# Shifting every right-hand tile of a fused retention and mixture-of-experts kernel by 32 bytes

## The chip, the cores and the metric

One core of one Trainium2 chip runs the whole program. The metric is the device time of one execution in microseconds (us). Engines are named as in the profile: PE is TensorE's matmul, PEld its weight load, DVE is VectorE, ACT is ScalarE, POOL is GpSimd and SP is SyncE, which issues the DMAs. On-chip memory (SBUF) has 128 partitions; a tile occupies the same byte range in each of them, and "address" below means the place in that range.

## The reference

Three stages follow each other on 1536 tokens (2 batches of 768) of width 512. Inputs and outputs are float32.

```python
# retention, 8 heads of width 64
state = gamma * state + outer(k[t], v[t])
y[t] = scale * q[t] @ state
# first layer, 512 -> 2048 -> 512
h = x @ w_in
x = (h * np.clip(h + 3.0, 0.0, 6.0) / 6.0) @ w_out
# second layer, 8 experts of 512 -> 1024 -> 512, all of them for each token
P = np.exp(x @ w_gate - max)
for _ in range(8):
    P /= P.sum(1, keepdims=True) + 1e-09
    P /= P.sum(0, keepdims=True) + 1e-09
    P *= N / E
for e in range(E):
    out += P[:, e:e + 1] * (np.maximum(x @ w1[e], 0.0) @ w2[e])
```

## The kernel before

A float32 product is made of three fp32r matmuls: each operand is split into a part `hi` and a rest `lo`, and hi·hi, hi·lo and lo·hi are added up in PSUM. A matmul takes its stationary operand (the weights, 128 x 128) by a weight load and then streams the moving operand, 512 or 384 columns wide. The order of all work is written by hand (`tc.manual_schedule`); each engine runs its instructions in that order.

The retention runs over 12 chunks of 128 tokens (`scores`, `attend`, `state`), and its output goes into `xhi`/`xlo`, one pair of tiles for each of three blocks of 512 tokens. The first layer has 48 steps: three groups of 4, 6 and 6 weight slices, and in each group blocks 0, 1 and 2 after one another. A step has 12 matmuls at L357 (`stage_a`: moving `xhi`/`xlo`, weights `whi`/`wlo`) and 12 at L387 (`stage_b`: moving `ghi`/`glo`, weights `whi`/`wlo`), all of them 512 columns wide; L357 runs two steps ahead. Its weights arrive as float64 and are split by DVE and ACT (`splitting`, L157 to L174) between the steps.

The second layer has two halves of 768 tokens, and for each 32 pairs of intermediate slices (64 in all). A pair makes 7 products of a Strassen-like scheme at L597 (`product`: 6 matmuls each, 384 columns, moving `xh`/`xl`, weights `w1hi`/`w1lo`), and between them come the matmuls at L672 (`outputs`: 512 columns, moving `w2hi`/`w2lo`, weights `gh`/`gl`) of the pairs before, 36 to a pair; the first two pairs have none beside them. DVE adds each finished L672 result into `o` (L685).

Tiles come from pools that take their bytes from the left or from the right end of the partition, in the order in which they are opened. The places in the built program of the kernel before are:

| side | pools and tiles | first byte of a tile, modulo 64 |
|---|---|---|
| left | `xo` (`x2`, `o`), `xa` (`xhi`, `xlo` of blocks 0 and 1: 43968, 52160, ...), `xf` (`xh`, `xl`), `m` (`raw0`, `s`, `w1hi`, `w1lo`) | 0 |
| left | the retention's `rs`, `qk`, `kv`, `a`, `ks`, `qs`, behind two tiles whose sizes are no multiples of 64 | 32 |
| right, from byte 229344 downwards | `sp` (`raw`, `w`, `t`), `xb` (`xhi`, `xlo` of block 2: 194528, 202720), `wp` and `wx` (`whi`, `wlo`), `gp` (`ghi`, `glo`), `m2` (`raw1`, `p`, `u`, `gh`, `gl`, `w2hi`, `w2lo`) | 32 |

`wx` is closed and `xf` and `m` are opened in the last block of the first layer; `m2` takes the place of `gp`, `wp`, `xb` and `sp` after the first layer. A tile that lies on bytes of an earlier one waits for that one's last reader.

Of the kernel before, what the change touches and what calls it, by code (L numbers as in the profile page):

```python
# [9 lines left out]
F32 = mybir.dt.float32  # L10
# [10 lines left out]
P = 128  # L21
# [34 lines left out]
def kernel(  # L56
# [20 lines left out]
    def pool(name, side, **kw):  # L77
        open_[name] = c = ExitStack()
        ctx.callback(c.close)
        return c.enter_context(tc.tile_pool(name=name, side=side, **kw))  # L80
# [2 lines left out]
    sk = pool("sk", "left", bufs=2)  # L83
    xo = pool("xo", "left", bufs=NU)
    xa = pool("xa", "left", bufs=NBLK - 1)
    sp = pool("sp", "right", bufs=3)
    xb = pool("xb", "right", bufs=1)
    wp = pool("wp", "right", bufs=NW)
# [826 lines left out]
```

## Time and profile before

| | before |
|---|---|
| median of 3 runs | 1346.34 us (1342.72 to 1346.85) |
| the profiled execution | 1346.3 us, span of its instructions 1344.5 us |
| PE busy | 98% of the span, 6766 matmuls |
| DVE busy | 68% |
| ACT busy | 42% |
| DMA | 99.69 MB on the hardware queue, 21.8% of 16 engines |
| granted TensorE clock | 0.999 |

Times in the views are microseconds from the first instruction of the span. A busy time of PE is modelled from pipelined matmuls, so that two neighbours overlap in it; how long a matmul holds the stream is the distance from its start to the next one's. The chain of waits is followed back from the last instruction, at each step to what released it; a piece "PE h L357 x12" is twelve matmuls at line 357 in a row, with the time from the first one's start to the start of the next piece.

### The profile page before, as it was taken

The page shows a single profiled execution, that of the slowest core. Times are in us where ns is not written, and L with a number is a line of the kernel's source. Part 1 is how long each engine was busy: PE and PEld are TensorE (multiplying, and loading weights), DVE is VectorE, ACT ScalarE, POOL GpSimd, SP SyncE. Part 2 cuts the span into 40 slices and gives each one's busy share as a digit, 9 for nine tenths or more (in the row PEclk, how much of TensorE's full clock was granted, in tenths as well). Part 3 has the DMA queues.
Part 4 walks back from the last instruction along what each step waited for, and adds up shares of the span by engine and source line. Part 5 has one row for each costly group of instructions (what it writes and reads, how often), then busy time and mean ns, then how long its engine had stood idle before and what let it go on. Part 6 is the DMA issues. An engine that isn't in the chain of part 4 may idle for free.

```text
span 1344.5 us, 17308 instructions
## 1 busy us (share of the span) xinstructions
PE 1323.4 (98%) x6766; PEld 1163.8 (87%) x6766; DVE 909.3 (68%) x1704; ACT 564.5 (42%) x1068; POOL 32.7 (2%) x34
## 2 busy tenths in 40 slices
PE   7899999999999999999999999999999999999998
PEld 6788788887888999999999998899999999999997
DVE  6866667438778666666666667766666666666663
ACT  3555545324543434433434434443443443443440
POOL 5300000000000000000000000000000000000000
PEclk9999999999999999999999999999999999999999
DMA  8622213000311111212111211311121211121201
GB/s 299 220 67 90 79 59 98 0 0 19 124 63 64 63 63 67 75 66 77 63 63 66 77 64 62 126 63 63 64 78 63 79 63 63 63 79 63 79 16 47
DMA packets 45533, 100.79 MB, mean 75 GB/s; under 512 B 3590, under 2 KB 4102, under 8 KB 45452
## 3 DMA queue, kind: packets, MB, share of 16 engines
q1 hardware_dynamic: 45452, 99.69, 21.8%
q8 instruction: 53, 0.87, 0.3%
q14 instruction: 28, 0.23, 0.1%
HBM read 96.53 MB, written 3.15 MB: 74 GB/s over the span
## 4 chain that ended last, share of the span: by engine, by line
PE 87%; DVE 7%; ACT 3%; issue 1%; DMA 1%; SPq 0%; ACTq 0%
PE acc L672 37%; PE h L597 33%; PE acc L387 8%; PE h L357 8%; ACT raw L164 1%; DVE raw L163 1%; DVE w L169 1%; DMA raw<-in_wf 1%; DVE w L159 1%; DVE a L297 0%; ACT t L365 0%; DMA raw<-in_we 0%; DVE xl L513 0%; DVE w1lo L513 0%; DVE w L157 0%
## 5 line engine op out<-in xcount | busy, mean ns | idle before, releaser
L597 PE MATMUL h<-xh,w1hi 128*128 128x384 f32 x896 | 302.0, 337 | 2.2 <-ACT p L616 1.5
L672 PE MATMUL acc<-w2hi,gl 128*128 128x512 f32 x768 | 301.7, 393 | 0.0
L597 PE MATMUL h<-xh,w1lo 128*128 128x384 f32 x896 | 301.1, 336 | 0.0
L597 PE MATMUL h<-xl,w1hi 128*128 128x384 f32 x896 | 300.6, 336 | 0.0
L672 PE MATMUL acc<-w2hi,gh 128*128 128x512 f32 x768 | 299.6, 390 | 0.0
L672 PE MATMUL acc<-w2lo,gh 128*128 128x512 f32 x768 | 298.8, 389 | 0.0
L685 DVE SCALAR_TENSOR_TENSOR o<-acc,pm,o 128x512 f32<-128x512 f32 x174 | 130.6, 750 | 143.8 <-PE acc L672 143.8
L597 PEld LDWEIGHTS h<-xh,w1hi 128*128 128x128 f32 x896 | 168.3, 188 | 21.7 <-ACT p L616 2.7
L597 PEld LDWEIGHTS h<-xl,w1hi 128*128 128x128 f32 x896 | 168.2, 188 | 19.4
L672 PEld LDWEIGHTS acc<-w2hi,gl 128*128 128x128 f32 x768 | 144.2, 188 | 30.9
L597 PEld LDWEIGHTS h<-xh,w1lo 128*128 128x128 f32 x896 | 168.2, 188 | 0.0
L672 PEld LDWEIGHTS acc<-w2lo,gh 128*128 128x128 f32 x768 | 144.3, 188 | 13.0
L672 PEld LDWEIGHTS acc<-w2hi,gh 128*128 128x128 f32 x768 | 143.9, 187 | 13.0
L616 ACT ACTIVATE p<-h 128x384 f32<-128x384 f32 x128 | 63.0, 492 | 202.9 <-PE h L597 202.8
L513 DVE TENSOR_TENSOR w1lo<-raw,w1hi 128x512 fp32r<-128x512 f32 (+1 forms) x128 | 71.1, 555 | 77.7 <-ACT w1hi L512 77.6
L513 DVE TENSOR_TENSOR w1lo<-s,w1hi 128x512 fp32r<-128x512 f32 x128 | 88.0, 688 | 38.5 <-ACT w1hi L512 38.3
L616 ACT ACTIVATE u<-h 128x384 f32<-128x384 f32 x64 | 31.5, 492 | 173.6 <-PE h L597 164.3
L607 ACT ACTIVATE gh<-p 128x384 fp32r<-128x384 f32 x128 | 66.7, 521 | 57.4 <-DVE p L615 57.4
L513 DVE TENSOR_TENSOR w2lo<-raw,w2hi 128x512 fp32r<-128x512 f32 x128 | 87.3, 683 | 4.4 <-ACT w2hi L512 4.4
L607 ACT ACTIVATE gh<-u 128x384 fp32r<-128x384 f32 x64 | 33.7, 526 | 127.5 <-DVE u L615 127.5
L512 ACT ACTIVATE w1hi<-s 128x512 fp32r<-128x512 f32 x128 | 79.7, 624 | 2.8 <-DVE s L532 1.4
L357 PE MATMUL h<-xhi,whi 128*128 128x512 f32 x192 | 76.6, 399 | 0.4 <-DVE t L367 0.4
(110 smaller groups left out, 1703.6 us busy)
## 6 DMA issues: line engine op xcount, KB each, us to landing
raw<-in_we SPq DMA_DIRECT2D x128, 512.0 KB, 3.4
raw<-in_wf SPq DMA_DIRECT2D x32, 512.0 KB, 3.7
kv<-in_kv SPq DMA_DIRECT2D x12, 512.0 KB, 5.7
qk<-in_qk SPq DMA_DIRECT2D x11, 512.0 KB, 5.8
out<-o SPq DMA_DIRECT2D x12, 256.0 KB, 2.0
qk<-in_qk SPq DMA_DIRECT2D x2, 256.0 KB, 3.2
gk<-in_gk SPq DMA_DIRECT2D x1, 24.0 KB, 3.4
tab<-in_tab SPq DMA_DIRECT2D x1, 16.5 KB
```

The source lines that it names most:

```text
L159: nc.vector.scalar_tensor_tensor(out=w, in0=hw, scalar=0x80000000, in1=w, op0=ALU.bitwise_and, op1=ALU.bitwise_or)
L163: nc.vector.tensor_scalar(out=top, in0=top, scalar1=0x7FFF, scalar2=None, op0=ALU.bitwise_and)
L164: nc.scalar.activation(out=top, in_=top, func=AF.Relu, bias=ebias, scale=1.0)
L357: nc.tensor.matmul(h, w[:, ks], x[:, k], start=(n == 0), stop=(n == 3 * KT - 1))
L387: nc.tensor.matmul(acc_b[i], l, r, start=(f == 0 and j == 0), stop=(f == nf - 1 and j == 2))
L512: nc.scalar.activation(out=hi, in_=t, func=AF.Copy)
L513: nc.vector.tensor_tensor(out=lo, in0=t, in1=f32(hi), op=ALU.subtract)
L597: nc.tensor.matmul(bank[:, 0:SB], l[:, w, ks], r[:, k], start=(start and n == 0), stop=(stop and n == 5), skip_group_check=True,)
L607: nc.scalar.activation(out=hi, in_=t, func=AF.Relu)
L616: copy = lambda out, a: nc.scalar.activation(out=out, in_=a, func=AF.Copy)
L672: nc.tensor.matmul(acc, l[:, cs], r[:, f % 2], start=(f == 0 and k == 0), stop=(f == 3 and k == 2))
L685: nc.vector.scalar_tensor_tensor(out=o[:, tt], in0=acc, scalar=sc, in1=o[:, tt], op0=ALU.mult, op1=ALU.add)
```

## The change

One tile of 128 partitions x 8 float32 (32 bytes) is allocated from the right before any other pool of that side. Nothing writes or reads it, and its pool stays open to the end. Every tile allocated from the right lies 32 bytes lower.

```diff
@@ -83,6 +83,8 @@
     sk = pool("sk", "left", bufs=2)
     xo = pool("xo", "left", bufs=NU)
     xa = pool("xa", "left", bufs=NBLK - 1)
+
+    pool("off", "right", bufs=1).tile([P, 8], F32, name="off")
     sp = pool("sp", "right", bufs=3)
     xb = pool("xb", "right", bufs=1)
     wp = pool("wp", "right", bufs=NW)
```

## Rows read from the trace of the kernel before

**Rows 1.** The page: busy time of each engine, and the chain's shares.

```profile
PE 1323.4 (98%) x6766; PEld 1163.8 (87%) x6766; DVE 909.3 (68%) x1704; ACT 564.5 (42%) x1068; POOL 32.7 (2%) x34
PE 87%; DVE 7%; ACT 3%; issue 1%; DMA 1%; SPq 0%; ACTq 0%
PE acc L672 37%; PE h L597 33%; PE acc L387 8%; PE h L357 8%; ACT raw L164 1%; DVE raw L163 1%; DVE w L169 1%; DMA raw<-in_wf 1%; DVE w L159 1%; DVE a L297 0%; ACT t L365 0%; DMA raw<-in_we 0%; DVE xl L513 0%; DVE w1lo L513 0%; DVE w L157 0%
```

**Rows 2.** Busy time by stretch: engines with counts, granted clock, DMA share, GB/s.

```profile
964.77:1322.04 357.27, 357.27 (x1796) 323.48 (x1795) 238.11 (x453) 142.55 (x296) 0.00 (x0) 1.00 0.18 62
94.67:143.19 48.52, 47.20 (x205) 37.79 (x204) 31.80 (x53) 28.73 (x42) 0.00 (x0) 1.00 0.23 76
0.00:66.60 66.60, 53.87 (x560) 45.31 (x561) 52.02 (x74) 27.92 (x47) 32.66 (x34) 1.00 0.73 262
```

**Rows 3.** The chain in the first layer: start, duration, what.

```profile
228.93 2.80 PE h L357 x12
231.73 2.75 PE acc L387 x12
...
256.66 2.80 PE h L357 x12
...
295.49 2.72 PE h L357 x12
298.21 2.72 PE acc L387 x12
300.93 2.72 PE h L357 x12
```

**Rows 4.** The chain through one pair of the second layer, and a later pair.

```profile
964.77 2.05 PE acc L672 x9
966.82 1.04 PE h L597 x6
967.87 1.37 PE acc L672 x6
969.23 1.04 PE h L597 x6
970.28 0.69 PE acc L672 x3
...
980.30 2.05 PE acc L672 x9
...
1306.50 2.05 PE acc L672 x9
```

**Rows 5.** PE's instructions in time, from the first layer to the second.

```profile
335.94 0.40 PE L387 MATMUL acc<-ghi,wlo 128*128 128x512 f32 x1
336.17 0.34 PE L597 MATMUL h<-xh,w1hi 128*128 128x384 f32 x1
336.35 0.34 PE L597 MATMUL h<-xl,w1hi 128*128 128x384 f32 x1
336.52 0.34 PE L597 MATMUL h<-xh,w1lo 128*128 128x384 f32 x1
...
341.90 0.33 PE L597 MATMUL h<-xh,w1hi 128*128 128x384 f32 x1
```

**Rows 6.** The chain where it leaves PE and where it returns.

```profile
91.92 2.76 PE acc L387 x12
94.67 0.02 issue
...
142.71 0.43 ACT x L402
143.14 0.04 issue
143.19 2.82 PE acc L387 x11
```

**Rows 7.** DVE by line and shape: busy, mean ns, idle before.

```profile
L513 DVE TENSOR_TENSOR w2lo<-raw,w2hi 128x512 fp32r<-128x512 f32 x128 | 87.3, 683 | 4.4 <-ACT w2hi L512 4.4
L513 DVE TENSOR_TENSOR w1lo<-raw,w1hi 128x512 fp32r<-128x512 f32 x64 | 44.3, 692 | 77.7 <-ACT w1hi L512 77.6
```

## The prediction

> **What bounds the kernel now.** I read the page's shares first. TensorE (PE) is busy 98% of the span, VectorE (DVE) 68%, ScalarE (ACT) 42%, and the chain that ended last lies on PE for 87% of its length, nearly all of it in four lines: L672 and L597 (second layer), L387 and L357 (first layer) [rows 1]. Then I read busy time by stretch. In the last 357 us before the closing run PE is busy for all of 357.27 us at clock 1.00, while DVE has a third of the stretch free; in the first 66.6 us PE is idle a fifth of the time and the DMA engines are 73% busy; from 94.67 to 143.19 us PE has 1.3 us of idle time [rows 2]. So from 143 us on nothing but the pace of the matmul stream counts: what a single matmul costs from start to start, times their number. Ahead of that, PE is not what ends last everywhere.
>
> The chain, read in order of time, has that pace in it. Twelve matmuls of 512 columns at L357 take 2.72 us in the steps of token block 2, that is 226.7 ns each, and 2.80 us in the steps of blocks 0 and 1, 233.3 ns each. L387 right behind them takes 2.72 and 2.75 us [rows 3]. Shape, type, instruction, clock and weights are the same. What differs is where `xhi`/`xlo` lie: block 2 is in `xb`, from the right, 32 bytes past a multiple of 64, as the weights are; blocks 0 and 1 are in `xa`, from the left, on multiples of 64. So in the dear steps the moving operand and the weights differ by 32 bytes modulo 64, and in the cheap ones they agree. A step (12 + 12) costs (256.66 - 228.93) / 5 = 5.546 us when mixed, and 300.93 - 295.49 = 5.44 us when not: 0.106 us more, 6.7 ns for each L357 matmul and some 25 ns over the first few L387 matmuls behind them.
>
> In the second layer L597 has both operands on the left (multiples of 64) and L672 both on the right (32 past). One pair of intermediate slices holds 7 products of 6 at L597 and 36 matmuls at L672 (9+6+3+6+3+6+3), and its period is (1306.50 - 964.77) / 22 = 15.533 us [rows 4]. L597 alone, with no L672 between, runs 32 intervals from 336.35 to 341.90 us, 173.4 ns each [rows 5]; a 512-column matmul at its best takes 226.7 ns [rows 3]. The floor of a pair is then 42 x 0.1734 + 36 x 0.2267 = 15.444 us. The 0.089 us above it is 12.8 ns for each of 7 trips from L672 to L597 and back. Where it lies can be seen at 335.94 us: the last 512-column matmul before an L597 takes 0.23 us and the first L597 0.18 us, where 0.17 follow [rows 5].
>
> **The change part by part.** The new tile is neither written nor read: no instruction, no DMA, no wait is added, and no queue's order is touched. What it does is move every tile allocated from the right (`sp`, `xb`, `wp`, `gp`, `wx`, `m2`) down by 32 bytes, to a multiple of 64. Left tiles stay, and so do the attention tiles that lie 32 past on the left (`rs`, `qk`, `kv`, `a`, `ks`, `qs`), so that attention's matmuls keep their operands. Where left and right regions are reused one after the other, one overlap goes: the second `w1lo` buffer began 32 bytes inside a `wlo` buffer of `wx`. That weight belongs to the second group, whose last reader is done when the third begins at 228.93 us [rows 3], and `w1lo` is written in the third group's last block; nobody waits there, 0 us. The narrowest gap between the two sides, 1056 bytes, becomes 1024.
>
> *First layer.* All operands of L357 and L387 agree modulo 64 afterwards, and by the rows the 32 mixed steps (8, 12 and 12 in the three groups) come down by 0.106 us each. From 143.19 us on, 21 of their L357 blocks lie on the chain: 21 x 0.106 = 2.2 us. The six blocks before 94.67 us give 0.6 us to PE, but there the chain goes over to ACT and DVE, which split weights, and comes back at 143.19 us [rows 6]. How much of the 0.6 us they pass on is not shown; between 0 and 0.6 I take 0.3. The five blocks between lie under that chain and give nothing: PE only waits longer at its end.
>
> *Second layer.* If the 12.8 ns of a round trip come from the change of alignment, all of it goes: 62 pairs (64 less the first two, which have no L672 beside them) x 0.089 = 5.5 us, all on the chain.
>
> *Other engines.* DVE's difference w1lo, all on the left, takes 692 ns and w2lo, all on the right, 683 ns [rows 7]. So leaving the odd 32 bytes costs a DVE instruction between 0 and 9 ns. That is hidden under PE, except where DVE is on the chain from 94.67 to 143.19 us: about 32 DVE instructions x 9 ns = 0.3 us at most. I take 0. For DMA I take 0 too: its share is 0.18 where PE bounds [rows 2].
>
> *What no row shows* is a 512-column stream on a multiple of 64 with weights on one as well, which is what L357, L387 and L672 all become. The nearest row from one side is L597 (both on multiples of 64, 384 columns), which runs at 173.4 ns. That is 13.4 ns over 384 columns at 2.4 GHz, and 226.7 is 13.3 ns over 512: the same floor. From the other side there are the mixed L357 steps, the only 512-column streams now on a multiple of 64, at 6.7 ns more. I take the first, since L597 agrees with the coming state in both operands and differs in width only. The second end is rival three.
>
> The sum: 2.2 + 0.3 + 5.5 = 8.0 us. The profiled execution took 1346.3 us with a span of 1344.5, and the median of the runs is 1346.34, so the one sum stands for both: 1346.3 - 8.0 = 1338.3 us.
>
> **The rivals.** *One: only the first layer gains.* The extra time at L672/L597 might come with the change of width from 512 to 384 columns, not with the addresses. For this speaks that the way back, from L597 to L672, changes alignment as much and costs nothing that shows: six L597 take 1.04 us, 173.3 each, last one included [rows 4]. Against it: the delay sits in the interval ahead of the first narrow matmul, when only its weights are being loaded [rows 5], and it is as large as in the mixed steps, where no width changes. Then 2.5 us go: 1343.8 us. Half of it would leave 1341.
>
> *Two: addresses do not matter,* and the 0.08 us between the L357 blocks come from something else that token block 2 has. Against it, three groups of blocks follow each other with the same weights, and only the place of `x` changes. Time: 1346.3 us. The Trainium skill speaks for this one: "SBUF — State Buffer", section "Who interferes with whom", says that PE has two independent read ports, one for the moving operand and one for the weights, and never waits on anyone. By that rule the 32 bytes are worth nothing. The trace does not agree with it in the mixed steps, 233.3 against 226.7 ns [rows 3].
>
> *Three: slower.* What is dear may be a 512-column stream that begins on a multiple of 64, whatever the weights; blocks 0 and 1 fit this as well as they fit the mixture. Then the change carries it to every such stream: 2304 at L672, 576 at L387 and 192 of block 2 at L357, 3072 x 6.7 ns = 20.6 us, all on PE: 1367 us. It decides as soon as the price is over 8.0 us / 3072 = 2.6 ns a matmul. Against it: L597's streams begin on multiples of 64 too and run at the floor.
>
> **How the numbers follow.** Both alignments matched, all gains: 0.60, 1338.3 us, with 1336 to 1342 for the terms that may come in part. First layer only: 0.22, 1343.8. Nothing: 0.08, 1346.3. Slower: 0.10, 1367. A measurement of this kernel can tell about 0.3%, or 4 us, from no change. So faster 0.60 (the likeliest case, its part gains included), same 0.30 (2.5 us is 0.19%, and the case of nothing), slower 0.10. The range 1335.5 to 1345 holds the first two, 0.82, with half a microsecond below and a microsecond above for the run's own scatter.
>
> **What would show it.** Right: L357 blocks of 12 take 2.72 us in all steps, L387 too; the period of a pair falls from 15.53 to 15.44 us; DVE and ACT rows move by less than 10 ns; PE's idle time around 140 us grows by about half a microsecond. Rival one: 2.72 in the first layer, 15.53 in the second. Rival three: 2.80 everywhere in the first layer, and nine L672 matmuls take 2.10 instead of 2.05 us. The prediction is wrong, too, if a DVE or DMA duration moves by more than these bounds where DVE is on the chain.

## The result, and the profile after

| | before | after |
|---|---|---|
| median of 6 runs each | 1344.61 us (1342.42 to 1346.85) | 1353.38 us (1350.64 to 1355.55) |
| ratio, 95% interval | | 1.0063 [1.0043, 1.0083] |
| profiled execution | 1346.3 us, span 1344.5 us | 1350.6 us, span 1348.9 us |
| first `xhi`/`whi` matmul of the first layer, us from the start | 66.35 | 61.62 |
| from there to the first matmul of the second layer | 269.8 us | 267.5 us (-2.3) |
| from there to the end of the second layer | 1004.2 us | 1015.7 us (+11.5) |

The change is a loss of 8.8 us by the medians, where a gain of 8 was forecast. (Lines of the kernel after stand two lower: L357 is L359, L387 L389, L597 L599, L672 L674.) The two profiled executions differ by 4.3 us only, because the stretch ahead of the first layer, whose matmuls the change leaves alone, ended 4.7 us earlier in the one of after. Over all the profiled kernels told of here that moment lies between 61.2 and 66.4 us, with no regard to where the tiles are. So from here on the two layers are compared by their own lengths: -2.3 + 11.5 = +9.2 us, which is the medians' difference within their scatter.

The page of after: busy time of each engine, the chain's shares, and one group of matmuls.

```profile
PE 1332.7 (99%) x6766; PEld 1169.2 (87%) x6766; DVE 906.1 (67%) x1704; ACT 565.0 (42%) x1068; POOL 31.9 (2%) x34
...
PE 88%; DVE 7%; ACT 3%; issue 1%; DMA 1%; SPq 0%; DVEq 0%; ACTq 0%
...
L674 PE MATMUL acc<-w2hi,gl 128*128 128x512 f32 x768 | 304.5, 396 | 0.0
```

The same instructions, the same bound [rows 1]: PE has 9.3 us more to do with the same 6766 matmuls, and ACT has 0.5 us more, DVE and POOL none.

The chain of after in the first layer, in order of time (start, duration, what), against [rows 3]:

```profile
228.56 2.72 PE h L359 x12
231.28 2.72 PE acc L389 x12
...
321.09 8.16 PE acc L389 x36
```

From 163 us on the steps of all three token blocks are cheap, those of blocks 0 and 1 too, except that in the last four, as before, other matmuls stand between. 36 matmuls at L389 in 8.16 us are 226.7 ns each.

The chain of after through one pair of the second layer, against [rows 4]:

```profile
964.65 2.08 PE acc L674 x9
966.73 1.06 PE h L599 x6
967.79 1.39 PE acc L674 x6
969.18 1.04 PE h L599 x6
970.23 0.70 PE acc L674 x3
970.92 1.06 PE h L599 x6
...
1310.63 2.08 PE acc L674 x9
1326.36 18.42 PE acc L674 x81
```

Nearly every kind of run has grown by 10 to 30 ns: nine L674 from 2.05 to 2.08 us, six from 1.37 to 1.39, three from 0.69 to 0.70, and the L599 behind nine and behind three from 1.04 to 1.06; those behind six still take 1.04. The closing run of 81, with no L599 in it, takes 18.42 us, and before it took 18.37: in the trace its first nine matmuls take 41 ns more than nine at 226.7, and from the tenth on nothing is added. The period of a pair is (1310.63 - 964.65) / 22 = 15.726 us, 0.193 us above that of before, and 62 pairs x 0.193 = 12.0 us. The whole second layer is 11.5 us longer, so this is the loss. Over the floor of 15.444 us a round trip between the two lines costs 0.282 / 7 = 40 ns, where it cost 12.8.

### The profile page after: what moved, and what is told of

Its sections match the earlier page's. It is cut to its first block, busy times and chain, and to the rows that moved or that the text cites. A ratio compares the mean times of both kernels' runs of the same rounds, so it can differ in the third digit from the quotient of the medians.

```text
span 1348.9 us, 17308 instructions
## 1 busy us (share of the span) xinstructions
PE 1332.7 (99%) x6766; PEld 1169.2 (87%) x6766; DVE 906.1 (67%) x1704; ACT 565.0 (42%) x1068; POOL 31.9 (2%) x34
## 4 chain that ended last, share of the span: by engine, by line
PE 88%; DVE 7%; ACT 3%; issue 1%; DMA 1%; SPq 0%; DVEq 0%; ACTq 0%
PE acc L674 38%; PE h L599 34%; PE acc L389 8%; PE h L359 8%; ACT raw L166 1%; DVE raw L165 1%; DVE w L171 1%; DMA raw<-in_wf 1%; DVE w L161 0%; DVE xl L515 0%; ACT t L367 0%; DVE t L369 0%; DVE w L159 0%; DVE a L299 0%; ACT xhi L339 0%
## 5 line engine op out<-in xcount | busy, mean ns | idle before, releaser
L674 PE MATMUL acc<-w2hi,gl 128*128 128x512 f32 x768 | 304.5, 396 | 0.0
L599 PE MATMUL h<-xh,w1hi 128*128 128x384 f32 x896 | 301.8, 337 | 2.2 <-ACT p L618 1.5
L674 PE MATMUL acc<-w2lo,gh 128*128 128x512 f32 x768 | 303.6, 395 | 0.0
L599 PE MATMUL h<-xl,w1hi 128*128 128x384 f32 x896 | 303.3, 338 | 0.0
L599 PE MATMUL h<-xh,w1lo 128*128 128x384 f32 x896 | 302.3, 337 | 0.0
L674 PE MATMUL acc<-w2hi,gh 128*128 128x512 f32 x768 | 298.8, 389 | 0.0
L599 PEld LDWEIGHTS h<-xh,w1hi 128*128 128x128 f32 x896 | 168.3, 188 | 24.1 <-ACT p L618 2.8
L599 PEld LDWEIGHTS h<-xl,w1hi 128*128 128x128 f32 x896 | 168.0, 187 | 19.5
L674 PEld LDWEIGHTS acc<-w2hi,gl 128*128 128x128 f32 x768 | 143.9, 187 | 30.9
L599 PEld LDWEIGHTS h<-xh,w1lo 128*128 128x128 f32 x896 | 168.2, 188 | 0.0
L674 PEld LDWEIGHTS acc<-w2hi,gh 128*128 128x128 f32 x768 | 144.3, 188 | 15.2
L674 PEld LDWEIGHTS acc<-w2lo,gh 128*128 128x128 f32 x768 | 144.0, 187 | 15.5
L359 PE MATMUL h<-xhi,whi 128*128 128x512 f32 x192 | 75.9, 395 | 0.8 <-DVE t L369 0.7
```

The lines of the kernel that those rows point to most:

```text
L359: nc.tensor.matmul(h, w[:, ks], x[:, k], start=(n == 0), stop=(n == 3 * KT - 1))
L599: nc.tensor.matmul(bank[:, 0:SB], l[:, w, ks], r[:, k], start=(start and n == 0), stop=(stop and n == 5), skip_group_check=True,)
L674: nc.tensor.matmul(acc, l[:, cs], r[:, f % 2], start=(f == 0 and k == 0), stop=(f == 3 and k == 2))
```

## Experiments

The first theory after the result, A in the expectations: the cost belongs to the change from a 384-column to a 512-column stream and back on PE, and its size goes by how the operands of the two lie to each other; with equal places it is dearer than with 32 bytes between. The rival, B: PE alone would not show it; with both sides on multiples of 64 the accesses of other engines and PE's meet more often. A predicts that the two halves of the change can be had apart, one a gain and one a loss.

**Matmul streams alone.** PE runs blocks of six matmuls with a weight load each from one tile of constants, and nothing else but a few DMA writes of zeros runs (one execution, as with the later streams). The letter gives the distance in steps of 8 bytes: `wide` and `slim` put the weights that far behind the moving operand; `turn` alternates six of 384 with six of 512 columns whose operands, both, lie that far from those of the narrow ones (a to h 0 to 56 bytes, i 64, j 96, k 128, l 160); `awide` and `aslim` keep one width and alternate between places 32 bytes apart. In `block(t, n, m, w)` n is the width, m and w are the places of the moving operand and of the weights in float32 elements of 4 bytes.

```
for _ in range(6): block(t, n, 0, d)                          # wide, slim
for _ in range(8): block(t, 384, 0, 0); block(t, 512, d, d)   # turn
for _ in range(8): block(t, n, 0, 0); block(t, n, 8, 8)       # awide, aslim
```

> This program leaves out the whole computation: it writes zeros and runs only matmul streams on constant data, with no ACT, DVE or DMA work beside them. Names: wide (512 columns) and slim (384 columns), letters a to h: the moving operand stays, the weights lie 0, 8, ... 56 bytes further modulo 64, 36 matmuls each. turn, letters a to l: 8 rounds of 6 matmuls of 384 columns at offset 0 and 6 of 512 columns with both operands at offset 0, 8, 16, 24, 32, 40, 48, 56, 64, 96, 128, 160 bytes. awide and aslim: both blocks of one width, at offsets 0 and 32. Theory A (it is the places of the streams against each other that count, at a change of width above all): turna (offset 0) costs about 41 ns a round over 6 x 173.3 + 6 x 226.7 = 2400 ns, turne (32) about 13 ns, as in the two kernels, and the offsets between them differ; widea and widee differ by 6.7 ns a matmul. Theory B (work of other engines at the same memory made the second layer slower): turna and turne are alike within 3 ns a round, and nothing but wide depends on the offset.

The chain of this kernel: start, duration, what.

```profile
30.58 8.16 PE widea L68 x36
38.74 8.30 PE wideb L68 x36
...
63.73 8.40 PE widee L68 x36
...
97.32 6.25 PE slima L68 x36
...
122.42 6.26 PE slime L68 x36
128.68 6.46 PE slimf L68 x36
...
147.70 19.46 PE turna L68 x96
...
226.10 19.32 PE turne L68 x96
...
304.35 19.41 PE turni L68 x96
...
382.14 22.11 PE awide L68 x96
404.25 16.88 PE aslim L68 x96
```

The floor of eight rounds is 48 x (0.1733 + 0.2267) = 19.20 us. With equal places (`turna`) a round costs 0.26 / 8 = 33 ns more, with 32 bytes between (`turne`) 15. So A holds, with no other engine running, and B falls. The size is short of the kernel's 40 ns; the table at the end of the experiments says why. Two more things stand here. `awide` lies 22.11 - 96 x 0.2267 = 0.35 us over its floor, 44 ns for each change of place and back, though the width never changes; `aslim` 0.24 us, 30 ns. So a change of width costs, a change of place costs, and the two at once, 32 bytes apart, cost least. And `widee`, (8.40 - 8.16) / 36 = 6.7 ns more a matmul, is the mixed step of [rows 3] without anything around it, while 384 columns don't mind 32 bytes (`slime`) but do mind 40 (`slimf`, 6 ns). The Trainium skill, "SBUF — State Buffer", section "Who interferes with whom", gives PE two independent read ports, one for the moving operand and one for the weights; `widee` differs from `widea` in the weights' place alone and is 6.7 ns a matmul dearer, so in these rows the one operand's place is not without effect on what the other costs.

**The first layer alone.** The tile's pool is closed with the first layer's, so that `m2` lies 32 past again.

```diff
-        for name in ("gp", "wp", "xb", "sp"):
+        for name in ("gp", "wp", "xb", "sp", "off"):
```

> The 32-byte tile is there in retention and first layer, and is given back before the second layer's right-hand tiles are allocated, so these lie where they lay before. Theory A (agreement of moving operand and weights pays in the first layer; in the second the 32 bytes between the L597 and the L672 operands were worth having): L357 blocks of 12 take 2.72 us, the period of a pair goes back to 15.53 us, and the time is 2 to 3 us under the kernel before: ratio 0.998. Rival (the tile itself or the places of the first layer set off the loss in some other way): period stays near 15.73 us, ratio 1.006.

Measured 1342.97 us against 1345.19, ratio 0.9981 [0.9971, 0.9990]. The first layer takes 267.5 us as after, the second 1005.0. Chain, an L359 block of the first layer and two pairs of the second:

```profile
235.58 2.72 PE h L359 x12
...
1286.27 2.05 PE acc L674 x9
1301.80 2.05 PE acc L674 x9
```

The gain of the prediction's first part is there at its full size, with the old period of 15.53 us.

**The second layer alone.** On the kernel before, the same tile is allocated just ahead of `m2`.

```diff
+        pool("off", "right", bufs=1).tile([P, 8], F32, name="off")
         pools["m2"] = pool("m2", "right", bufs=2, reuse_waits="tile")
```

> The 32-byte tile is allocated only ahead of the second layer's right-hand tiles; retention and first layer lie as before. Theory A: L357 blocks of token blocks 0 and 1 take 2.80 us as before, the period of a pair is 15.73 us, and the time is 62 x 0.194 = 12 us over the kernel before: ratio 1.009. Rival (as for the run before): period 15.53 us, ratio 1.000.

Measured 1354.25 us, ratio 1.0076 [1.0059, 1.0093]; first layer 269.7 us, second 1015.7, period 15.73:

```profile
968.09 2.08 PE acc L672 x9
...
1314.07 2.08 PE acc L672 x9
```

(1314.07 - 968.09) / 22 = 15.73 us. The two halves add up to the change: each layer has the length that it has in the kernel after. By the medians it is -2.2 + 9.1 = 6.9 us against 8.8, where the three intervals reach 1.3, 2.3 and 2.7 us to either side.

**Every distance up to 248 bytes.** Streams alone again: six rounds of 6 x 384 and 6 x 512 columns, both operands of the wide ones 8 x k bytes past those of the narrow ones (`by`, two letters for k, eight to a letter); `sb` has in addition the narrow stream's weights 32 bytes past its moving operand, `sa` and `sc` 16 and 48. It asks whether the distance modulo 64 is all that counts (A1) or the distance itself (A2).

```
for _ in range(6): block(t, 384, 0, w); block(t, 512, 2 * k, 2 * k)
```

> This program leaves out the whole computation, as the streams before: only matmul streams on constant data. Each name is 6 rounds of 6 matmuls of 384 columns and 6 of 512 columns; the floor of a round is 2400 ns. by + two letters: both 512-column operands lie 0, 8, 16, ... 248 bytes past the 384-column ones modulo 256 (byaa is 0, byae 32, bybe 96). sa, sb, sc + two letters: the 384-column weights are moved as well, by 16, 32 and 48 bytes, and the 512-column operands by 0 to 56. Theory A1 (the offset counts modulo 64): the 32 values of by repeat every 8, with the lowest, 13 ns, at 32, 96, 160 and 224. Theory A2 (the offset counts in 8-byte steps without that period; where a round begins in the sequence counts too): 32 gives 13 ns, 96 and 160 give some 33, and there may be offsets under 13.

```profile
30.95 14.62 PE byaa L68 x72
45.57 14.79 PE byab L68 x72
...
89.77 14.50 PE byae L68 x72
...
148.45 14.56 PE byba L68 x72
...
207.23 14.62 PE bybe L68 x72
...
383.17 14.49 PE byda L68 x72
...
441.66 14.51 PE byde L68 x72
...
676.18 14.44 PE sbae L68 x72
```

Over the floor of 14.40 us, by round: 37 ns at 0 bytes, 65 at 8, 17 at 32, 27 at 64, 37 at 96, 15 at 192, 18 at 224. There is no period of 64 bytes: 0, 64 and 192 differ, and so do 32 and 96. A1 falls here. 32 bytes, the place of the kernel before, is among the cheapest of the 32, and `sbae`, with the narrow stream's weights moved as well, is the cheapest of all, 7 ns. These means hold the first round, which comes in from the block before; without it, from start to start in the trace, 0 bytes cost 33 ns, 32 bytes 13.3 and `sbae` 6.7.

**Half the changes.** On the kernel after, chunks of nine L674 are given out at every second slot, so that a pair has 4 round trips and not 7.

```diff
-                    while done * 16 < (chunks - alone) * slot:
+                    while slot % 2 == 0 and done * 16 < (chunks - alone) * slot:
```

> The changed kernel, with the L674 matmuls of a pair let in behind every second product instead of each one: 4 changes between the widths and back in a pair instead of 7, the same matmuls otherwise. Theory A (the loss sits at the changes, some 41 ns a round trip at offset 0): 3 x 41 ns x 62 pairs = 7.6 us less than the changed kernel, and 5 at least, since longer runs let a transient run out further: about 1346 us, ratio 1.001. Rival (each 512-column matmul from these places is dearer, wherever it stands): no gain, ratio 1.006.

Measured 1352.37 us against 1342.86, ratio 1.0073 [1.0053, 1.0093]. The expectation missed: the second layer takes 1014.6 us, 1.1 less than after.

```profile
967.84 2.08 PE acc L674 x9
969.92 2.10 PE h L599 x12
972.03 2.08 PE acc L674 x9
```

A round trip of 9 and 12 takes 972.03 - 967.84 = 4.19 us over a floor of 4.12, some 66 ns; a pair has 4 x 66 = 264 ns of it instead of 282. At equal places the price isn't paid at the change itself but spread over the matmuls behind it. From start to start in the trace, nine L674 take 229, 233, 236, 224, 231, 236, 228, 233 and 231 ns, 41 over nine at 226.7; a run that ends after three has paid 18 of them, after six 29. The L599 behind a run of nine pay 26 ns within six matmuls, be they six or twelve. The kernel after has one such trip in a pair already, at 67 ns, with six cheaper ones beside it. Here all four trips are of the dear kind, and so half the changes cost nearly as much.

**Both together: first layer alone and half the changes.** With 32 bytes between, where little is spread.

> The kernel with the 32-byte tile in retention and first layer only, and the L674 matmuls behind every second product. Theory A: a round trip costs 13.3 ns there, so 3 x 13.3 ns x 62 = 2.5 us less than without the regrouping: ratio 0.996. Rival (bunching makes the products wait for ACT to free their banks): PE shows idle time at L599, ratio 0.998 or more.

The edits are those of the two diffs above. Measured 1340.25 us against 1342.86, ratio 0.9972 [0.9961, 0.9982]; the second layer takes 1002.2 us, 2.8 less than with the first layer alone.

```profile
964.35 2.05 PE acc L674 x9
966.40 2.08 PE h L599 x12
968.48 2.05 PE acc L674 x9
```

4.13 us for the same round trip, 13 ns over the floor in the trace, so the products wait for nothing: 62 pairs x 3 trips saved x 13.3 ns are 2.5 us, and 2.8 were measured.

**The weights of the first matrix moved as well.** The cheapest case of the streams put to use: on the last kernel, a 32-byte tile ahead of `w1hi` and `w1lo`.

```diff
+        if "w1off" not in pools:
+            pools["w1off"] = pools["m"].tile([P, 8], F32, tag="w1off", name="w1off", bufs=1)
```

> As the kernel with the tile in retention and first layer only and half the switches, and the second layer's left-hand weights w1hi and w1lo moved up by 32 bytes, so that xh and xl alone stay at a multiple of 64 there. Theory A2 (as the offsets measured on bare streams say: 6.7 ns a round trip with the 384-column weights and both 512-column operands 32 bytes past the 384-column moving operand, against 13.3): 4 x 6.6 ns x 62 = 1.6 us less than without it, period of a pair 15.47 us: ratio 0.996. Rival (the bare streams don't carry over, since DVE and ACT work at the same memory): period 15.50 us or more.

Measured 1337.31 us against 1342.93, ratio 0.9958 [0.9945, 0.9971], the second layer 1000.6 us, 1.6 less again. The lines of this kernel are L676 and L601:

```profile
965.56 2.04 PE acc L676 x9
967.60 2.09 PE h L601 x12
969.69 2.04 PE acc L676 x9
```

1.6 us / (62 x 4) = 6.5 ns for each round trip, as 13.3 against 6.7 in the streams said. By its ratio this version is faster than both kernels of the case. Among the last three versions the intervals of neighbours overlap, and the differences of 2.8 and 1.6 us are read from one trace each.

**Other sizes of the tile.** On the kernel after, 96 and 64 bytes. Against the left tiles the right ones lie at 0 modulo 64 with 96 bytes, as after, and 64 bytes below the equal place; with 64 bytes they lie at 32 modulo 64, as before, and 32 below.

```diff
-    pool("off", "right", bufs=1).tile([P, 8], F32, name="off")
+    pool("off", "right", bufs=1).tile([P, 24], F32, name="off")
```

> The changed kernel with one number changed: the tile at the right end has 96 bytes instead of 32. Both sides lie at multiples of 64 as in the changed kernel, the right one 64 bytes lower still (192 modulo 256 past the left one). Theory A2: bare streams cost 13.3 ns a round trip there, not the 33 of offset 0, so the period of a pair is near 15.53 us and not 15.73, the L359 blocks stay at 2.72 us if the first layer's rule goes modulo 64, and the time is 2 to 3 us under the kernel before: ratio 0.998. Theory A1 (all multiples of 64 are alike): as the changed kernel, ratio 1.006.

> The changed kernel with a tile of 64 bytes: the right-hand tiles lie 32 past a multiple of 64 as in the kernel before, but 64 bytes lower (224 modulo 256 past the left ones instead of 32). Theory A2: L359 blocks of token blocks 0 and 1 take 2.80 us if that rule goes modulo 64; bare streams cost 20 ns a round trip at 224 against 13.3 at 32, so the period of a pair is 15.58 us and the time 7 x 6.7 ns x 62 = 2.9 us over the kernel before: ratio 1.002. Theory A1 (only the place modulo 64 counts): as the kernel before in both, ratio 1.000.

96 bytes: 1349.30 us against 1342.93, ratio 1.0036 [1.0024, 1.0049]. The chain, a step of the first layer and two pairs:

```profile
231.50 2.77 PE acc L389 x12
234.27 2.76 PE h L359 x12
...
1294.57 2.05 PE acc L674 x9
1310.16 2.05 PE acc L674 x9
```

64 bytes ([P, 16]): 1346.71 us, ratio 1.0026 [1.0015, 1.0037]:

```profile
230.77 2.80 PE h L359 x12
233.57 2.76 PE acc L389 x12
...
1290.32 2.05 PE acc L674 x9
1305.90 2.05 PE acc L674 x9
```

With 64 bytes the period is 1305.90 - 1290.32 = 15.58 us, 19 ns a round trip, which is the streams' price at 224 (that is -32) bytes; it is not before's 15.53, though modulo 64 nothing differs. With 96 bytes it is 15.59 us, 21 ns a round trip, where A1 wanted after's 40 and the streams at 192 (-64) bytes 13 to 15: between both, and the expectation of 15.53 us missed. The first layer says the same. Steps of 2.76 and 2.77 us, for operands that agree modulo 64, are neither the 2.72 of agreement nor the 2.80 of 32 bytes.

The traces say where the rest lies. The price of a round trip over 226.7 and 173.3 ns a matmul, from start to start, median of all pairs, by the number of L674 in it (six L599 follow), beside that of the bare streams without their first round:

| kernel (distance in the streams' terms) | nine | six | three | streams, six and six |
|---|---|---|---|---|
| before (32 bytes) | 13 ns | 13 ns | 13 ns | 13 ns |
| after (0) | 67 ns | 33 ns | 40 ns | 33 ns |
| tile of 64 bytes (224) | 20 ns | 20 ns | 20 ns | 20 ns |
| tile of 96 bytes (192) | 13 ns | 13 ns | 33 ns | 13 ns |

With six and six the kernels cost what the streams cost, in all four. What differs from the streams is in the trips with three or nine, and these make the kernel after's 40 and this one's 21: (67 + 3 x 33 + 3 x 40) / 7 = 41, and (4 x 13 + 3 x 33) / 7 = 22, within the rounding of the floor. So A2 holds with one addition: the price goes by the distance and, at some distances, by the number of L674 before the change back.

## Why the prediction was wrong, point by point

**The bound: right.** From 143 us on only the matmul stream's pace counted. All of the loss is in start-to-start distances of matmuls; no engine but PE has more than 0.5 us more to do.

**The first layer: right in mechanism and size.** 2.5 us were forecast, 2.3 came by the trace, and 2.2 by the medians with the first layer alone. By parts, the stretch from the chain's return to PE (143.19 us before, 138.00 after) to the second layer gave 1.9 us where 2.2 were forecast: the first four L359 blocks behind the return take between 2.76 and 2.90 us in both kernels, and the gain comes from the 17 others. The steps before the chain goes over to ACT and DVE gave 0.4 where 0.3 were taken. The rule behind it was too wide, though: not "equal modulo 64" makes a step cheap, for with the right side 64 bytes further down, at 0 modulo 64 still, L359 costs 2.76.

**The second layer: the step that failed.** It is "If the 12.8 ns of a round trip come from the change of alignment, all of it goes". -5.5 us were forecast, +11.5 came. Two readings led to it. The mixed steps of the first layer showed that 32 bytes between moving operand and weights cost 6.7 ns, within one matmul. That was carried over to 32 bytes between two matmuls that follow each other, which is another thing: the bare streams have the first at 6.7 ns more a matmul, and the second, together with a change of width, at 15 ns a round trip where equal places cost 33. And the excess of 12.8 ns was read against a floor that no change measured here reached; the cheapest, `sbae`, still costs 7. In the trace of before, every change between 512 and 384 columns is also a change of place: L672 to L597 by 32 bytes in each of the seven trips, and at 335.94 us L387 to L597 as well [rows 5]. So a change of width at equal places, which is what all 434 round trips were to become, had no row. The prediction bounded the new stream from both sides (a 512-column stream on multiples of 64, rival three) and not the new change between streams; its bounds for that were 0 and 12.8 ns, where 40 came. The 32 bytes were what made the change cheap.

**Evidence that spoke against it and weighed too little.** The prediction had seen that the way back changes places as much and costs nothing that shows, and that some 25 ns lay over the first L387 matmuls behind the mixed ones, where the width is the same. Both fit a price that belongs to a pair of streams and runs on into the later one.

**The rivals.** One was nearest in mechanism: the extra time does come with the change of width. But it kept the 12.8 ns as they were (1343.8 us), and so did not end on the other side. Two falls by the first layer. Three had the sign, 1367 us, with the wrong mechanism: `widea`, a 512-column stream on a multiple of 64 with its weights there too, runs at the floor (8.16 us for 36), and L359 and L389 do so in the kernel. That choice, the first end for the streams, was right.

**Other engines: right.** DVE's difference over `w2hi`, on the right, takes what it took in [rows 7], and ACT's busy time is 565.0 us against 564.5.

```profile
L515 DVE TENSOR_TENSOR w2lo<-raw,w2hi 128x512 fp32r<-128x512 f32 x128 | 87.3, 683 | 4.5 <-ACT w2hi L514 4.5
```

**The idle time that was to grow: right in sign.** The stretch in which ACT and DVE bound the kernel, 94.67 to 143.19 us in [rows 2], lies from 89.53 to 138.00 us after and is as long within 0.05 us. PE is busy in it for 46.84 us and idle for 1.63, where it was idle for 1.32: 0.3 us more, of the half a microsecond that was forecast.

```profile
89.53:138.00 48.47, 46.84 (x205) 37.78 (x204) 31.80 (x53) 28.70 (x42) 0.00 (x0) 1.00 0.24 77
```

**What stays open.** What in PE or in its reads makes one distance dearer than another was not settled; there is a table of prices by distance, and a transient behind each change. The streams ran with six and six alone, so that the prices of trips with three and nine are known from the kernels only, and why the L599 pay 26 ns behind nine L674, 4 behind six and 22 behind three in the kernel after is open.

## What to carry to other kernels

Look up whether the state that a change leads to occurs anywhere in the trace as it will be, the neighbours of each instruction included; where it does not, a price of zero is one end of a range, and the other end is a rival of its own. Where PE is the bound and two streams alternate, try a few start offsets between them, and between weights and moving operand, on bare streams first, with the lengths of the kernel's own runs: two small programs here led to the shifted weights, 1.6 us or 0.1%, which no reading of the first trace had. Fewer alternations pay in full only where each run is already longer than the transient behind a change (13 ns for each trip left out, with 32 bytes between); where the runs are shorter than it, longer ones pay more of it (1.1 us for 186 trips fewer, at equal places). So price distance and length together.

## What the runs showed of the hardware

- The pace of a matmul depends on where its operands start: 512 columns with weights 32 bytes behind the moving operand take 233.3 ns instead of 226.7, with 8 bytes 230.6 (8.30 us / 36); 384 columns take the same at 0 and 32 bytes.
- A change between streams costs something even if no wait is involved. Per round trip of width, six and six, first round included: 65 ns at 8 bytes, 37 at 0, 17 at 32, 7 with the narrow stream's weights moved too. Without the first round most of these prices are multiples of 6.7 ns: 6.7, 13.3, 20, 33, 40, 47, 53, 60, 67. Per round trip of place alone, at one width: 44 ns for 512 columns, 30 for 384.
- At equal places the price is spread over the matmuls behind the change, up to nine of 512 columns (41 ns) and six of 384 (26 ns): a round trip with runs of 9 and 12 costs 66 ns, one with runs of 3 to 9 and 6 costs 40 on average. With 32 bytes between, 8 of the 13 ns lie in the distance from the last wide matmul to the first narrow one (235 ns for 226.7), and the length of the runs makes no difference.
